# Position tables: two instead of four, filled in long rows from one tile

## The chip, the cores and the metric

The kernel runs on one core of a Trainium2 chip. The metric is the time of one execution on the device in microseconds (us), as the median of some runs. All inputs lie in the chip's memory (DRAM below); the core works from its on-chip memory (SBUF, 128 partitions) and the accumulators of the matrix engine (PSUM). Its engines are PE (matrix multiplication), DVE (vector), ACT (activation), POOL (general) and SP (which here issues DMA transfers). Sixteen DMA engines move the data.

## What is computed

Three steps on 4608 tokens (8 batches of 576):

```
attn_out = attention of q on p', where p' = attention of the 32 packed queries p on k, v
x = silu(attn_out @ w_in) @ w_out          # 512 -> 2048 -> 512
# top-1 mixture of 8 experts
e_idx = argmax(x @ w_gate)                 # one expert for each token
out[token] = gate_w * sigmoid(x @ w_output_gate)[e_idx] * (relu(x @ w1[e_idx]) @ w2[e_idx])
```

The last step gathers the tokens of one expert. That needs a list, made on the chip, of which token stands at which place.

## The kernel before

**Batches.** `batch(b)` runs over the 16 hidden slices f of the middle layer: `mm1` (L664) computes a slice, `act` (L673, L674) applies the activation, `split_hi` and `split_lo` (L679, L684) split it into a coarse and a fine part, and `mm2` (L715) multiplies with `w_out` two slices later. Between these steps the attention of the next batch is run by `att_steps` (s1 to s9; s3 is the product with v at L579, and L581 scales it). The code of `batch` is the order of the instructions on every engine; nothing is moved by a planner, and each engine runs its own instructions strictly in that order.

**First batch.** `w_in` and `w_out` come as 64-bit words and are converted during batch 0: `f64_load` (L432) loads 512 KB into a tile of tag stg, and `f64_conv` does three DVE operations on it (L452, L455, L458), for `w_out` into a tile of tag wf with two buffers, which ACT and POOL then split (L469, L470). A load reuses a stg buffer when DVE has read it. `load_att` (L524) fetches k, v and q of the next batch; the second half of v, for batch 1, is issued in step 5 and used by s3 in step 7.

**Position tables.** Four tables `perm` in DRAM hold, for each of 8 x 36 x 128 places (and 128 spare ones), one row of 16 integers, the first of which counts. `setup_late`, in batch 0 after step 4, fills each table: the first with 4608, the others with 0. The source is a tile of 289 columns, broadcast 16 times for each partition; the first table has a tile of its own, the other three share one, both of tag wf. Each fill is one DMA on SP's queue of 2312 KB (2048 rows of 1156 bytes). A row of zeros (`zrow`) is written to the end of `xr`, the rows of x in DRAM.

**Scatters.** After the routing of a group of 4 or 5 blocks of 128 tokens, `put` (L782) writes, on POOL's queue, the token numbers of each block to the places computed for them. Block i goes to table i % 4, so a scatter follows another to the same table after three others. The value written is the token for table 0, and the token less 4608 for the others.

**Gathers.** In the expert stage 38 pairs of a block of places and an expert run one after the other. `fetch_ix` reads, on SP, the 128 places of a block from all four tables into `xix_p`, and POOL adds the four (L911, L912). The sum is the token, or 4608 for an empty place, which points to the row of zeros. `fetch_x` (L920) gathers the rows of x, and `trx` (L948) transposes them on PE. The first three pairs fetch early, in batch 7; pairs 3 to 5 fetch after the last block is placed.

**Queues.** SP issues its DMAs in order through eight semaphores in turn, so each waits until the eighth before it has landed. In the rows of the order below a DMA's waits stand in brackets: DMAHW0 to DMAHW7 are those eight semaphores, DMASW0 to DMASW7 those of POOL's DMAs, and an engine's name its own progress.

Of the kernel before, what the change touches and what calls it, by code (L numbers as in the profile page):

```python
# [8 lines left out]
F32 = mybir.dt.float32  # L9
# [3 lines left out]
I32 = mybir.dt.int32  # L13
ALU = mybir.AluOpType
# [10 lines left out]
E8 = 8  # L25
F2 = 1024
NTOK = B * S
NBLK = NTOK // 128
CAP = NBLK
NPAIR = NBLK + E8 - 1  # L30
XW = DM + 1
# [3 lines left out]
HS = S // 2  # L35
EARLY = 3
NSTATIC = NBLK + 2
NPERM = 4
PW = 16


def constants():
    p = np.arange(128)
    c = np.zeros((128, C_END), np.float32)
    c[:, C_ID:C_ID + 128] = np.eye(128)
    e = np.arange(E8)
    c[:, C_E:C_E + E8] = e
    c[:, C_OFF:C_OFF + E8] = (e - E8) * CAP
    c[:, C_LT:C_LT + E8 * E8] = (e[None, :] < e[:, None]).reshape(1, -1)
    c[:, C_J] = p  # L50
    k = np.full((128, 256), 0x3F80, np.uint16)
    k[:, :128] *= p[:, None] < p[None, :]
    t = np.stack([block_tokens(i) for i in range(NBLK)], axis=1).astype(np.int32)
    t[:, np.arange(NBLK) % NPERM > 0] -= NTOK
    t = np.concatenate([t, np.zeros((128, PW - 1), np.int32)], axis=1)
    return {"cst": c, "cstk": k, "cstt": t}

# [9 lines left out]
def block_tokens(i):  # L67
    return np.concatenate([np.arange(t, t + n) for _, t, n in block_spans(i)])
# [13 lines left out]
class Kernel:  # L82
    def __init__(self, tc, ins, out):
# [3 lines left out]
        self.ws2 = nc.dram_tensor("ws2", (E8, 4, 2, 128, 2 * DM), F32, kind="Internal").ap()  # L87
        self.perm = [nc.dram_tensor(f"perm{i}", ((E8 * CAP + 1) * 128, PW), I32, kind="Internal").ap() for i in range(NPERM)]
        self.xr = nc.dram_tensor("xr", (NTOK + 1, XW), F32, kind="Internal").ap()
# [76 lines left out]
    def setup_late(self):  # L166
        nc = self.nc
        nc.sync.dma_start(self.tri, self.i["cstk"].bitcast(BF16).rearrange("p (a b) -> p a b", a=2))
        nc.sync.dma_start(self.tok, self.i["cstt"])
        nc.gpsimd.memset(self.nt_run, 0.0)  # L170
        for i, perm in enumerate(self.perm):
            if i < 2:
                fill = self.stg.tile([128, E8 * CAP + 1], I32, tag="wf", bufs=2, name="fill")
                nc.gpsimd.memset(fill, 0 if i else NTOK)
            nc.sync.dma_start(perm.rearrange("(p c) w -> p (c w)", p=128).rearrange("p (w c) -> p w c", w=PW),
                              fill.unsqueeze(1).to_broadcast([128, PW, E8 * CAP + 1]))
        z = self.rt.tile([128, 5, XW], F32, tag="xr", name="zrow")[:1, 0]
        nc.gpsimd.memset(z, 0.0)
        nc.sync.dma_start(self.xr[NTOK:NTOK + 1, :], z)

    def pick(self):
        assert self.group is None and not self.late
# [575 lines left out]
    def place(self, g):  # L758
# [15 lines left out]
        def put():  # L774
# [6 lines left out]
            for r in range(n):  # L781
                nc.gpsimd.indirect_dma_start(  # L782
                    out=self.perm[(i0 + r) % NPERM], out_offset=bass.IndirectOffsetOnAxis(ap=di[:, r:r + 1], axis=0),
                    in_=self.tok[:, i0 + r:i0 + r + PW], in_offset=None)
# [114 lines left out]
    def fetch_ix(self, j):  # L899
        nc = self.nc  # L900
        if j < EARLY:
            off = nc.values_load(self.ptab[0:1, 1 + j:2 + j], engines=[ENG.SP], min_val=0, max_val=E8 * CAP * 128)
            self.ex[j] = self.estar
        else:
            off = nc.values_load(self.tab[0:1, 0, j:j + 1], engines=[ENG.SP], min_val=0, max_val=E8 * CAP * 128)
            self.ex[j] = nc.values_load(self.tab[0:1, 1, j:j + 1], engines=[ENG.SP], min_val=0, max_val=E8 - 1)
        ix = self.rt.tile([128, NPERM + 2], I32, tag="xix_p", bufs=4, name="xix_p")
        at = self.rt.tile([128, 1], I32, tag="xix", bufs=6, name="xix")
        for i, perm in enumerate(self.perm):
            nc.sync.dma_start(ix[:, i:i + 1], perm[bass.ds(off, 128), 0:1])  # L910
        nc.gpsimd.tensor_tensor(out=ix[:, 4:6], in0=ix[:, 0:2], in1=ix[:, 2:4], op=ALU.add)  # L911
        nc.gpsimd.tensor_tensor(out=at, in0=ix[:, 4:5], in1=ix[:, 5:6], op=ALU.add)  # L912
        return at.bitcast(U32)

    def flag(self, j):
# [100 lines left out]
def layouts(q, k, v, p, moe_w_in, moe_w_out, moe2_w_gate, moe2_w_output_gate, moe2_w1, moe2_w2):  # L1016
    def headmajor(x):
        return np.ascontiguousarray(x.reshape(B, 4, 2, S, D).transpose(0, 2, 4, 1, 3).reshape(B, 128, 4, S))

    vv = np.zeros((B, 640, H, D), v.dtype)  # L1020
    vv[:, :S] = v.transpose(0, 2, 1, 3)
    vv = vv.reshape(B, 5, 128, 4, 2, D).transpose(0, 4, 2, 1, 3, 5)
    return {
        "q": headmajor(q), "k": headmajor(k), "v": np.ascontiguousarray(vv).reshape(B, 2, 128, 5, 256),
        "p": np.ascontiguousarray(p.reshape(B, 4, 2, NP, D).transpose(0, 2, 4, 1, 3)).reshape(B, 128, 4, NP),
        "w_in": np.ascontiguousarray(moe_w_in).view(np.int64), "w_out": np.ascontiguousarray(moe_w_out).view(np.int64),
        "wgt": np.ascontiguousarray(moe2_w_gate.reshape(4, 128, E8).transpose(1, 0, 2)), "wog": np.ascontiguousarray(moe2_w_output_gate.T),
        "w1": np.ascontiguousarray(moe2_w1), "w2": np.ascontiguousarray(moe2_w2),
        **constants(),
    }  # L1030
# [19 lines left out]
```

## Time and profile before

| | |
|---|---|
| median of 3 runs | 1361.1 us (1360.93 to 1362.29) |
| profiled execution | 1360.51 us, of which the span of the instructions is 1358.7 us |
| PE busy | 1269.3 us (93% of the span) |
| DVE, ACT, POOL busy | 653.9, 505.8, 173.4 us |
| granted clock of PE, mean | 0.971 |

Times in the rows below are us from the span's start. A granted clock of 1.00 is PE's full speed (2.4 GHz), 0.50 half of it (1.2 GHz). A matmul counts as busy from its start to its modelled end. The share of the DMA engines is the mean busy share of the sixteen and can exceed 1 a little.

### The profile page before, as it was taken

What the parts mean: (1) busy time and instruction counts of PE and PEld (TensorE: products, weight loads), DVE (VectorE), ACT (ScalarE), POOL (GpSimd) and SP (SyncE); (2) the same over time, 40 slices, a digit from 0 to 9 for tenths busy, and PEclk for the clock granted to TensorE, in tenths of its full rate; (3) what the DMA queues carried; (4) which work ended last, traced back from release to release, by engine and by line L of the source; (5) the groups of instructions that cost most, each with busy time, mean ns of one, the idle gap of its engine ahead of it and who ended that gap; (6) DMA issues with size and microseconds to landing.
All of it is one profiled execution on the core that took longest, in us unless ns stands there. A gap on an engine that the chain in (4) does not pass through costs nothing. (4 is left out here: it accounts for less than half of the span.)

```text
span 1358.7 us, 24463 instructions
## 1 busy us (share of the span) xinstructions
PE 1269.3 (93%) x8414; PEld 1020.1 (75%) x8416; DVE 653.9 (48%) x1417; ACT 505.8 (37%) x980; POOL 173.4 (13%) x236
## 2 busy tenths in 40 slices
PE   7754699999999899999999999999999999999997
PEld 3543578778788688787787788878888888888886
DVE  6953965845865745857556745232222222222221
ACT  3321255445464444454454433223223222222322
POOL 0220310100010100101000111112212212211210
PEclk9686899999999999999999999999999999999999
DMA  7598346846695855776665414442557383722630
GB/s 292 205 233 210 110 151 222 274 158 223 211 292 180 257 197 189 227 285 209 225 219 193 104 32 157 108 127 71 193 173 249 121 301 97 277 66 69 236 129 23
DMA packets 118303, 247.72 MB, mean 182 GB/s; under 512 B 30177, under 2 KB 56609, under 8 KB 118178
## 3 DMA queue, kind: packets, MB, share of 16 engines
q1 hardware_dynamic: 110946, 226.35, 51.0%
q0 software_dynamic: 7232, 19.72, 4.4%
q8 instruction: 77, 1.26, 0.4%
q14 instruction: 48, 0.39, 0.1%
HBM read 401.92 MB, written 96.29 MB: 367 GB/s over the span
## 5 line engine op out<-in xcount | busy, mean ns | idle before, releaser
L715 PE MATMUL acc<-wo,ghi 128*128 128x512 f32 x1024 | 320.9, 395 | 0.0
L715 PEld LDWEIGHTS acc<-wo,ghi 128*128 128x128 f32 x1024 | 194.5, 190 | 39.0
L664 PE MATMUL ps_h<-a,m_hi 128*128 128x288 f32 x1024 | 215.5, 303 | 0.8 <-DVE a L630 0.8
L715 PE MATMUL acc<-wo,glo 128*128 128x512 f32 x512 | 212.9, 416 | 0.0
L664 PE MATMUL ps_h<-a,m_lo 128*128 128x288 f32 x512 | 163.5, 319 | 30.9 <-DVE g L674 25.2
L1007 PE MATMUL py<-queue_q_buf,hhi 128*128 x608 | 190.7, 395 | 0.0
L979 PE MATMUL pu<-queue_q_buf,xhi 128*128 x560 | 174.6, 393 | 0.0
L664 PEld LDWEIGHTS ps_h<-a,m_hi 128*128 128x128 f32 x1024 | 171.1, 196 | 2.7 <-DVE a L630 1.0
L993 DVE TENSOR_TENSOR hlo<-ph,hhi 128x512 fp32r<-128x512 f32 x76 | 49.0, 686 | 247.3 <-ACT hhi L992 247.3
L674 DVE SCALAR_TENSOR_TENSOR g<-g,ps_h 128x576 f32<-128x576 f32 x128 | 96.1, 751 | 131.0 <-ACT g L673 130.2
L673 ACT ACTIVATE g<-ps_h 128x576 f32<-128x576 f32 x128 | 83.3, 651 | 188.8 <-PE ps_h L664 186.0
L664 PEld LDWEIGHTS ps_h<-a,m_lo 128*128 128x128 f32 x512 | 99.8, 195 | 57.0 <-DVE g L674 33.3
L1007 PEld LDWEIGHTS py<-queue_q_buf,hhi 128*128 128x128 f32 x608 | 114.5, 188 | 25.6
L715 PEld LDWEIGHTS acc<-wo,glo 128*128 128x128 f32 x512 | 97.3, 190 | 43.0 <-issue 24.8
L1007 PE MATMUL py<-queue_q_buf,hlo 128*128 x304 | 122.9, 404 | 0.0
L979 PEld LDWEIGHTS pu<-queue_q_buf,xhi 128*128 128x128 f32 x560 | 105.3, 188 | 22.4
L782 POOL DMA_INDIRECT perm<-tok,dsti x36 | 38.9, 1081 | 647.9 <-DVE dsti L779 507.4
L679 ACT CAST ghi<-g 128x512 fp32r<-128x512 f32 x128 | 79.4, 620 | 107.6 <-DVE g L674 106.5
L979 PE MATMUL pu<-queue_q_buf,xlo 128*128 x280 | 113.7, 406 | 0.3 <-ACT hs L981 0.3
L981 ACT ACTIVATE hs<-pu 128x512 f32<-128x512 f32 x76 | 45.4, 598 | 164.2 <-PE pu L979 162.5
L684 DVE TENSOR_TENSOR glo<-g,ghi 128x512 fp32r<-128x512 f32 x128 | 88.5, 692 | 31.1 <-ACT ghi L679 26.2
L1012 POOL DMA_INDIRECT out<-y,xix x38 | 38.2, 1006 | 328.2 <-ACT y L1010 320.6
(183 smaller groups left out, 1501.1 us busy)
## 6 DMA issues: line engine op xcount, KB each, us to landing
queue_q_buf<-ws SPq DMA_DIRECT2D x70, 4096.0 KB
ws<-shi SPq DMA_DIRECT2D x64, 512.0 KB
mid<-in_w SPq DMA_DIRECT2D x48, 512.0 KB
ws<-mid SPq DMA_DIRECT2D x48, 512.0 KB
att_v<-in_v SPq DMA_DIRECT2D x15, 640.0 KB
perm<-fill SPq DMA_DIRECT2D x4, 2312.0 KB
og<-in_wog SPq DMA_DIRECT2D x35, 256.0 KB
att_k<-in_k SPq DMA_DIRECT2D x15, 576.0 KB
```

The costliest lines, as they stand in the source:

```text
L664: nc.tensor.matmul(ps[:, hf, :288], lw[:, qd, fs], rx[:, qd, ts], start=(i == 0), stop=(i == 5))
L673: nc.scalar.activation(out=g2, in_=ps[:, :, :288], func=AF.Tanh, scale=0.5)
L674: nc.vector.scalar_tensor_tensor(out=g2, in0=g2, scalar=1.0, in1=ps[:, :, :288], op0=ALU.add, op1=ALU.mult)
L679: self.nc.scalar.copy(out=hi, in_=self.graw[:, :512])
L684: self.nc.vector.tensor_tensor(out=lo, in0=self.graw[:, :512], in1=self.ghi.bitcast(F32), op=ALU.subtract)
L715: self.nc.tensor.matmul(acc, l, r, start=(first and i == 0), stop=(last and i == 2))
L782: nc.gpsimd.indirect_dma_start(out=self.perm[(i0 + r) % NPERM], out_offset=bass.IndirectOffsetOnAxis(ap=di[:, r:r + 1], axis=0), in_=self. ...
L979: nc.tensor.matmul(ps, l[:, ks], w[:, k, r, ns], start=(i == 0), stop=(i == 11))
L981: nc.scalar.activation(out=self.hs[j][:, n * 512:n * 512 + 512], in_=ps, func=AF.Relu)
L993: nc.vector.tensor_tensor(out=lo[:, n], in0=ps, in1=hi[:, n].bitcast(F32), op=ALU.subtract)
L1007: nc.tensor.matmul(ps, l[:, k // 4, ks], w[:, k // 2, r, (k % 2) * DM:(k % 2) * DM + DM], start=(i == 0), stop=(i == 23))
L1012: nc.gpsimd.indirect_dma_start(out=self.out, out_offset=bass.IndirectOffsetOnAxis(ap=ix[:, 0:1], axis=0), in_=y, in_offset=None, bounds_ch ...
```

## The change

There are two tables instead of four. Both are filled with 2304 (half of 4608) from one tile of 2312 columns that lies in the buffer of tag xr, so each partition writes 2 rows of 9248 bytes to each table (256 rows for a table). All token numbers are written less 2304, so that the sum of the two tables is the token, or 4608. The row of zeros is taken from the tile `zero` that the kernel holds already. Block i goes to table i % 2, and a gather reads two columns and adds them once.

```diff
-NPERM = 4
+NPERM = 2
...
-    t[:, np.arange(NBLK) % NPERM > 0] -= NTOK
+    t -= NTOK // NPERM
...
-        for i, perm in enumerate(self.perm):
-            if i < 2:
-                fill = self.stg.tile([128, E8 * CAP + 1], I32, tag="wf", bufs=2, name="fill")
-                nc.gpsimd.memset(fill, 0 if i else NTOK)
-            nc.sync.dma_start(perm.rearrange("(p c) w -> p (c w)", p=128).rearrange("p (w c) -> p w c", w=PW),
-                              fill.unsqueeze(1).to_broadcast([128, PW, E8 * CAP + 1]))
-        z = self.rt.tile([128, 5, XW], F32, tag="xr", name="zrow")[:1, 0]
-        nc.gpsimd.memset(z, 0.0)
-        nc.sync.dma_start(self.xr[NTOK:NTOK + 1, :], z)
+        n = (E8 * CAP + 1) * PW // 2
+        fill = self.rt.tile([128, 5 * XW], I32, tag="xr", name="fill")[:, :n]
+        nc.gpsimd.memset(fill, NTOK // NPERM)
+        for perm in self.perm:
+            nc.sync.dma_start(perm.rearrange("(p c) w -> p (c w)", p=128).rearrange("p (h n) -> p h n", h=2),
+                              fill.unsqueeze(1).to_broadcast([128, 2, n]))
+        nc.sync.dma_start(self.xr[NTOK:NTOK + 1, :].rearrange("o (p c) -> (o p) c", p=3), self.zero.bitcast(F32)[:3, :XW // 3])
...
-        ix = self.rt.tile([128, NPERM + 2], I32, tag="xix_p", bufs=4, name="xix_p")
+        ix = self.rt.tile([128, NPERM], I32, tag="xix_p", bufs=4, name="xix_p")
...
-        nc.gpsimd.tensor_tensor(out=ix[:, 4:6], in0=ix[:, 0:2], in1=ix[:, 2:4], op=ALU.add)
-        nc.gpsimd.tensor_tensor(out=at, in0=ix[:, 4:5], in1=ix[:, 5:6], op=ALU.add)
+        nc.gpsimd.tensor_tensor(out=at, in0=ix[:, 0:1], in1=ix[:, 1:2], op=ALU.add)
```

The lines of the changed kernel stand two lower from `setup_late` on (L430 for L432) and three lower from `fetch_ix` on (L917 for L920).

On SP, in batch 0 after step 4, this stands in a row before (perm is a table, stg a buffer of the weight loads, att_v the v of the next batch):

```order
37 L175 DMA perm<-fill 2048x1x289 [waits DMAHW4_49,Pool_49]
38 L175 DMA perm<-fill 2048x1x289 [waits DMAHW5_49,Pool_49]
39 L175 DMA perm<-fill 2048x1x289 [waits DMAHW6_49]
40 L175 DMA perm<-fill 2048x1x289 [waits DMAHW7_49]
41 L179 DMA xr<-zrow 1x513 [waits DMAHW0_49,Pool_49]
42 L432 DMA stg_401<-in_w_out 128x1024 [waits DMAHW1_49,DVE_49]
43 L432 DMA stg_401<-in_w_in 128x1024 [waits DMAHW2_49,DVE_49]
44 L524 DMA att_v<-in_v 128x1280 [waits DMAHW3_49,PE_49]
45 L432 DMA stg_401<-in_w_out 128x1024 [waits DMAHW4_49,DVE_49]
46 L432 DMA stg_401<-in_w_in 128x1024 [waits DMAHW5_49,DVE_49]
47 L432 DMA stg<-in_w_out 128x1024 [waits DMAHW6_49,DVE_49]
48 L432 DMA stg<-in_w_in 128x1024 [waits DMAHW7_49,DVE_49]
```

And in the changed kernel at the same place:

```order
37 L175 DMA perm<-fill 256x1x2312 [waits DMAHW4_49,Pool_49]
38 L175 DMA perm<-fill 256x1x2312 [waits DMAHW5_49]
39 L177 DMA xr<-zero 3x171 [waits DMAHW6_49]
40 L430 DMA stg_401<-in_w_out 128x1024 [waits DMAHW7_49,DVE_49]
41 L430 DMA stg_401<-in_w_in 128x1024 [waits DMAHW0_49,DVE_49]
42 L522 DMA att_v<-in_v 128x1280 [waits DMAHW1_49,PE_49]
43 L430 DMA stg_401<-in_w_out 128x1024 [waits DMAHW2_49,DVE_49]
```

Two fills are gone, the rows of those left are eight times as long, and att_v stands two places earlier behind them.

On POOL, at the start of the expert stage, the last two groups of blocks are scattered before the first list of the late pairs is added up (perm0 to perm3 are the tables, dsti the places of a group; the branch belongs to a loop over buffers):

```order
L782 DMA perm3<-tok_91,dsti_8436 36992x16 [waits DMASW6_49,DVE_49]
L782 DMA perm0<-tok_91,dsti_8436 36992x16 [waits DMASW7_49,DMASW3_49]
L782 DMA perm1<-tok_91,dsti_8436 36992x16 [waits DMASW4_49,DMASW0_49]
L782 DMA perm2<-tok_91,dsti_8436 36992x16 [waits DMASW5_49,DMASW1_49]
L935 UNCONDITIONAL_BRANCH
L782 DMA perm3<-tok_91,dsti_8575 36992x16 [waits DMASW2_49,DVE_49]
L911 TENSOR_TENSOR xix_p_8694<-xix_p_8694 128x2 [waits DMAHW6_49,DMAHW7_49,DMAHW1_49,DMAHW0_49]
L912 TENSOR_TENSOR xix_8695<-xix_p_8694 128x1 [waits Pool_49]
```

In the changed kernel:

```order
L780 DMA perm1<-tok_91,dsti_8421 36992x16 [waits DMASW0_49,DVE_49]
L780 DMA perm0<-tok_91,dsti_8421 36992x16 [waits DMASW3_49,DMASW1_49]
L932 UNCONDITIONAL_BRANCH
L780 DMA perm1<-tok_91,dsti_8421 36992x16 [waits DMASW4_49,DMASW2_49]
L780 DMA perm0<-tok_91,dsti_8421 36992x16 [waits DMASW5_49,DMASW3_49]
L780 DMA perm1<-tok_91,dsti_8560 36992x16 [waits DMASW4_49,DVE_49]
L909 TENSOR_TENSOR xix_8680<-xix_p_8679 128x1 [waits DMAHW7_49,DMAHW6_49]
```

The scatters stand in the same order but alternate between two tables, so the third, fourth and fifth each follow one to the same table two places ahead, and one of the two additions is gone.

## Rows read from the trace of the kernel before

**Rows 1.** Five stages: length, engines' busy us (instructions), PE clock, DMA share, GB/s.

```profile
68.00:84.00 16.00, 6.15 (x71) 5.02 (x69) 2.76 (x4) 1.39 (x3) 1.69 (x5) 0.82 1.04 239
84.00:103.00 19.00, 12.65 (x69) 9.86 (x69) 17.16 (x25) 6.39 (x14) 6.28 (x6) 0.86 1.10 228
103.00:123.00 20.00, 1.37 (x41) 1.23 (x41) 0.48 (x2) 0.00 (x0) 0.00 (x0) 0.50 1.06 260
123.00:180.00 57.00, 45.75 (x289) 35.17 (x290) 49.11 (x69) 19.80 (x40) 21.47 (x19) 0.88 0.35 118
180.00:1300.00 1120.00, 1102.65 (x7319) 896.37 (x7318) 518.46 (x1203) 441.56 (x852) 123.83 (x178) 1.00 0.56 186
```

**Rows 2.** Waits, 68 to 128 us: total us, times, longest.

```profile
PE ps_s L579 <- DMA att_v<-in_v: 21.2, 1, 21.2
```

**Rows 3.** Timeline of DVE in batch 0: start, us, engine, line, operation, [idle before].

```profile
67.42 2.30 DVE L569 TENSOR_SCALAR sm<-sm 128x2 f32<-128x2 f32 x1
...
83.09 0.43 DVE L452 TENSOR_SCALAR wf<-stg 128x512 uint32<-128x512 uint32 x1 [13.17 <-DMA perm<-fill]
...
89.20 0.69 DVE L458 SCALAR_TENSOR_TENSOR w_in<-stg,w_in 128x512 uint32<-128x512 uint32 x1
...
102.78 0.69 DVE L458 SCALAR_TENSOR_TENSOR w_in<-stg,w_in 128x512 uint32<-128x512 uint32 x1
122.99 0.28 DVE L581 TENSOR_SCALAR pp<-ps_s,sm 128x64 f32<-128x64 f32 x1 [19.52 <-PE ps_s L579]
...
126.89 0.75 DVE L674 SCALAR_TENSOR_TENSOR g<-g,ps_h 128x576 f32<-128x576 f32 x1 [1.83 <-ACT g L673]
```

**Rows 4.** Timeline of PE, step 7 to step 8 of batch 0.

```profile
99.80 0.61 PE L715 MATMUL acc<-wo,ghi 128*128 128x512 f32 x2
121.63 1.30 PE L579 MATMUL ps_s<-att_v,a1t 128*32 128x64 f32 x40 [21.21 <-DMA att_v<-in_v]
```

**Rows 5.** Timeline of SP's queue in batch 0: us is the issue alone.

```profile
68.99 23.88 SPq L175 DMA_DIRECT2D perm<-fill  x4
...
104.98 0.56 SPq L524 DMA_DIRECT2D att_v<-in_v  x1
...
117.82 0.33 SPq L432 DMA_DIRECT2D stg<-in_w_in  x1
```

**Rows 6.** Stretches under the fills, under 4 KB rows, under the xr rows.

```profile
70.00:116.00 46.00, 16.80 (x127) 13.08 (x125) 18.51 (x26) 7.04 (x15) 6.28 (x6) 0.74 1.10 223
190.00:195.00 5.00, 5.00 (x41) 3.93 (x41) 2.65 (x5) 4.17 (x9) 0.00 (x0) 1.00 1.05 419
824.00:828.00 4.00, 4.00 (x34) 3.41 (x33) 1.94 (x7) 1.42 (x3) 0.00 (x0) 1.00 0.96 258
```

**Rows 7.** By line: ns min/median/max, first to last start; two tiles' memsets, L569.

```profile
L174 POOL MEMSET fill<- x2: 348/348/349, 68.6 to 68.9; 128x289 int32 x2
...
L178 POOL MEMSET zrow<- x1: 522/522/522, 69.2 to 69.2; 1x513 f32 x1
...
L569 DVE TENSOR_SCALAR sm<-sm x8: 160/166/2297, 11.3 to 700.9; 128x2 f32<-128x2 f32 x8
```

**Rows 8.** Timeline of POOL, SP and PE, start of the experts.

```profile
869.23 0.96 POOL L782 DMA_INDIRECT perm<-tok,dsti  x1 [35.55 <-DVE dsti L779]
...
873.01 0.96 POOL L782 DMA_INDIRECT perm<-tok,dsti  x1 [0.31 <-issue]
...
881.96 0.95 POOL L782 DMA_INDIRECT perm<-tok,dsti  x1 [7.99 <-DVE dsti L779]
892.09 2.09 SPq L910 DMA_DIRECT2D xix_p<-perm  x4
...
900.15 0.63 PE L948 MATMUL px<-cst,x 128*128 128x128 f32 x4 [1.18 <-DVE hlo L993]
```

**Rows 9.** L782 by line: from issue to landing, whole span; then 868 to 880 us.

```profile
DMA to landing us min/median/max: 4.7/6.2/9.5
...
DMA to landing us min/median/max: 8.8/8.9/9.0
```

## Prediction

> **What bounds the kernel now.** I read the busy time by stage first [rows 1]. From 180 to 1300 us PE is busy for 1102.65 of 1120 us at a granted clock of 1.00: what is saved on SP, POOL or the DMA engines there is worth nothing unless PE waits for it. Before 180 us the kernel is in the first batch, and PE is not the bound. In 84 to 103 us DVE is busy for 17.16 of 19.00 us; in 103 to 123 us no engine does anything (PE 1.37, DVE 0.48 of 20 us) while the DMA engines are at a share of 1.06. So the reader should see two holes in the first batch, with a stretch between them and one after them in which DVE is the bound (49.11 of 57 us in 123 to 180).
>
> The waits and the DVE timeline name both [rows 2, 3]. The first hole: L452 starts at 83.09 after 13.17 us of idling, released by the landing of a fill. It writes a buffer of tag wf, and the two fill tiles have taken buffers of that tag. The second: PE finishes its accumulations of step 7 at 100.41 (99.80 and 0.61) and waits 21.21 us, to 121.63, for att_v [rows 4]; DVE, whose next work is L581 on that result, idles for 19.52 us, and 1.83 us more before L674.
>
> Why att_v is late is on the SP queue [rows 5]. The four fills are issued from 68.99 on, and SP is held for 23.88 us by that alone. att_v goes out at 104.98. The stg load at 117.82 could go only when the fourth fill had landed (in the order of SP it waits for the semaphore that this fill posts), so I put the end of the fills at 117.3; att_v, with the 1.0 MB of stg loads ahead of it, lands 4.3 us behind, at 121.6. The holes thus have one cause: 4 x 2312 KB of stores, written at 223 GB/s over 70 to 116 us while the engines' share is 1.10 [rows 6].
>
> **The change, part by part.**
>
> *The wf buffers.* The fill no longer takes one. L450, as L452 is called now, waits for its own source and POOL only, and both were there. DVE idle: minus 13.2 us.
>
> *The fill tile.* One POOL memset of 128x2312 takes the place of two of 128x289 (348 ns each) and one of 1x513 (522 ns) [rows 7]. From 289 to 513 columns the price grows by 174 ns, 0.78 ns a column; from 2312 columns I get 348 + 2023 x 0.78 = 1.9 us, an estimate from these rows. The three old memsets end at 69.7, the new one would end at 68.7 + 1.9 = 70.6. This is not free: L569, a 128x2 operation whose median is 166 ns, lasts 2.30 us there and ends at 69.72, when POOL's last memset ends [rows 3, 7]. I read it as held by POOL, so DVE gets free 1.0 us later. Bounds: 0 (if it was something else) and plus 1.5. I take plus 1.0. SP also starts the fills at about 70.7 instead of 68.99; that goes into the next term.
>
> *The fills.* 2 x 2312 KB = 4.73 MB instead of 9.47. The rate with rows of 9248 bytes stands in no row. The nearest: stores with rows of 1156 bytes, 223 GB/s, and of 2052 bytes (the xr rows, 1.03 MB in 4.00 us), 258 GB/s, both at a share near 1; 4 KB rows, stores and loads mixed, 419 GB/s [rows 6]. As time per row, the old fills took 46.5 us (70.8 to 117.3) / 8192 = 5.7 ns and the xr rows 4.0 us / 512 = 7.8 ns: a line through both gives 3.0 ns a row and 2.3 ps a byte, so 9248 bytes would take 24.6 ns and 512 rows 12.6 us (376 GB/s). The bounds are 223 and 419 GB/s, 21.2 and 11.3 us; I take 12.6, nearer to the 4 KB rows, because what the two slow rows share is a short row.
>
> When is att_v there? DVE gets to L452 at 70.9 (69.9, where it began to idle, and 1.0) instead of 83.09, so all of the DVE-bound stretch moves up by 12.2 us. SP can issue att_v once DVE's L458 (89.20 + 0.69 before, 77.7 now) has freed the stg buffer of the load ahead of it: about 78.4, inside the fills. The old fills, issued at 68.99, were moving some 2 us later; the new ones, issued at 70.7, would run from about 72.7 to 85.3, and att_v land 4.3 us later (as now: 117.3 to 121.6), at 89.6. PE asks for it at 100.41 - 12.2 = 88.2. DVE, though, has work to 102.78 + 0.69 - 12.2 = 91.3 [rows 3], and then 1.9 us of conversion before L674, so PE may start as late as 89.6 without any cost (1.3 us for L579, 1.6 for the next step at full clock, 0.7 for ACT). The stall comes out between 0 and 1 us; I take 0.8 left of 19.52 + 1.83 = 21.35. DVE idle: minus 20.5 us. With 223 GB/s the landing moves to 98.2, and 8.6 us of stall stay.
>
> The Trainium skill speaks against this term: by its page "DMA: Bandwidth & Descriptors", sections Specifications and Why small descriptors are slow, a transfer runs at line rate from 512 bytes on, and each packet costs about 3 cycles beside one per 32 bytes. By that, rows of 1156 bytes would already be within 8% of rows of 9248 (my estimate from its figures: 36 cycles and 3), and this term would shrink by 7.8 us. The rows of 223 and 419 GB/s [rows 6] disagree with it here, unless it is the bytes of a store that are slow; that is the first rival below.
>
> *The zero row.* It loses its POOL memset (in the numbers above) and its wait on POOL. Three short rows on the DMA engines: nothing.
>
> *Two tables.* Each scatter (L782) now waits for the last but one instead of the last but four. In batches 1 to 6 POOL has nothing else after it and nobody waits for the table. The last two groups matter [rows 8, 9]: four scatters at 869.23 to 873.01, landing 8.8 to 9.0 us after issue, then one at 881.96, and SP reads the tables at 892.09. Now the third goes at about 878.2, the fourth at 879.5. The fifth needs the third to have landed: 884.4 (at 6.2 us, the median of all scatters) to 887.2 (at 9.0), and lands itself 6.2 to 9.0 us later, at 890.6 to 896.2. The reads are delayed by 0 to 4 us. Against that the first lists need 2 reads instead of 4 (2.09 us of issue, so 1.0 less) and one POOL addition instead of two, and PE waits 1.18 us at 900.15 behind this chain. So this place gives minus 1.2 to plus 3.0 us; I take 0. The fetches of the early pairs in batch 7 are delayed too, but their rows are used twelve steps of that batch later.
>
> *Fewer reads.* 76 fewer on SP and 38 fewer additions on POOL: beside a PE that is busy for 1102.65 of 1120 us, nothing.
>
> **The sum** is made against the profiled execution, 1360.5 us (span 1358.7); the median of the runs is 1361.1. 1360.5 - 13.2 + 1.0 - 20.5 + 0 = 1327.8. I say 1328. From 123 us on the first batch is DVE-bound and then PE-bound, so nothing that I see takes the shift back.
>
> **The rivals.**
>
> *The fills stay slow by the byte.* If stores to this table run at 223 GB/s whatever the row, att_v lands at 98.2 and 8.6 us of stall remain where I put 0.8: 1336. For it: 2052-byte rows reach only 258. Against: 4 KB rows at 419. The page of the Trainium skill named above would have it so, that there is nothing to win by the row.
>
> *The scatters become the bound at the start of the experts.* The chain of [rows 8] at its upper end, beside the forecast: plus 3.0, and 1331. For it: 8.9 us of landing in this group. Against: the median over all scatters is 6.2 [rows 9], and at that the fifth has landed before SP asks.
>
> *Only the first hole closes.* The loads might be held by SP's buffers, not by the fills: then 1348. Against: the stall's releaser, and nothing else is on the DMA engines in 103 to 116 us.
>
> *Slower.* att_v stands in the queue behind the whole fill. Rows of 9 KB would have to be so slow that the stall left exceeds the 12.2 + 21.35 us won, that is, it lands after 89.6 + 33.6 = 123.2: 4.73 MB in 46.2 us (72.7 to 118.9), 102 GB/s. At 90 GB/s it would be 1367. No stage with stores runs below 223.
>
> **How the numbers follow.** Forecast 0.70, fills slow by the byte 0.15, scatters 0.08, first hole only 0.05, slower 0.02. The forecast's own range is 1324 to 1331 (all of the 21.35, the faster start of the experts and a quicker clock at one end; 2 us more of stall at the other). With the slow fills in, the range is 1323 to 1338: what lies outside is the fourth and fifth case and some of the edges. About 0.2% (2.7 us) is what a measurement of this kernel can tell from no change; faster by more than that holds in all cases but the last: 0.97, within 0.01, slower 0.02.
>
> **What would show it.** In the profile after: no idle of L450 before its first conversion behind the fill, and the 128x2 operation ahead of it lasting some 3.3 us; SP held for about 1 us by two fills; a DMA share near 1 from 73 to 85 us at over 350 GB/s; PE's wait for att_v at 1 to 2 us where it was 21.2; the first batch over 33 us earlier; the distance from the start of the steady stretch to the end unchanged within 2 us; scatters 6 to 9 us apart in pairs. I am wrong if the fills still take 20 us, or if a new wait of DVE or PE stands between 90 and 180 us.

## The result, and the profile after

The changed kernel takes **1328.3 us** (median of 4 runs, 1327.8 to 1329.6) where the kernel before takes 1361.0 on the same chip: a ratio of **0.976** (95% interval 0.9743 to 0.9777), 32.7 us less. The forecast was 1328. The profiled execution is 1328.53 us long, with a span of 1326.8. One of the four executions of rows1088 below took 1770.8 us at a mean granted clock of 0.65 and is left out of its median.

Five stretches of the profile after (columns as in [rows 1]: length, busy us of PE, PEld, DVE, ACT and POOL with instructions, granted clock, DMA share, GB/s):

```profile
72.00:84.00 12.00, 8.32 (x95) 6.47 (x85) 10.42 (x16) 4.52 (x10) 4.22 (x4) 1.00 1.01 392
74.00:86.00 12.00, 8.58 (x56) 6.23 (x56) 11.04 (x17) 3.88 (x9) 3.83 (x4) 1.00 1.00 384
84.00:92.00 8.00, 5.80 (x61) 4.41 (x62) 7.46 (x12) 1.87 (x4) 2.08 (x2) 0.87 1.03 400
112.00:130.00 18.00, 11.27 (x75) 7.75 (x74) 17.31 (x22) 6.05 (x13) 8.58 (x7) 0.95 0.05 18
147.00:1267.00 1120.00, 1103.43 (x7321) 897.35 (x7320) 518.92 (x1203) 441.08 (x852) 118.32 (x143) 1.00 0.55 186
```

Under the fills the DMA engines are as full as before (a share near 1) but move 384 to 400 GB/s instead of 223 [rows 6], and DVE is busy for 87 to 93% of these stretches. The steady 1120 us, shifted by 33, are what they were in [rows 1]. And in 112 to 130 us the DMA engines now have almost nothing to do, which the experiments use.

DVE in batch 0 (start, us, engine, line, operation, [idle before]); L567, L450, L579 and L672 are L569, L452, L581 and L674 of before [rows 3]:

```profile
67.09 1.25 DVE L567 TENSOR_SCALAR sm<-sm 128x2 f32<-128x2 f32 x1
...
68.46 2.15 DVE L450 TENSOR_SCALAR wf<-stg 128x512 uint32<-128x512 uint32 x1
70.65 0.69 DVE L453 SCALAR_TENSOR_TENSOR wf<-stg,wf 128x512 uint32<-128x512 uint32 x1
...
90.87 0.28 DVE L579 TENSOR_SCALAR pp<-ps_s,sm 128x64 f32<-128x64 f32 x1 [0.28 <-PE ps_s L577]
...
94.58 0.76 DVE L672 SCALAR_TENSOR_TENSOR g<-g,ps_h 128x576 f32<-128x576 f32 x1 [1.63 <-ACT g L671]
```

POOL at the same time, with the memset of the fill tile:

```profile
66.80 1.52 POOL L468 TENSOR_TENSOR wo<-wf,wo 128x512 fp32r<-128x512 f32 x1 [1.36 <-ACT wo L467]
...
68.30 2.03 POOL L173 MEMSET fill<- 128x2312 int32 x1
```

The 13.17 us ahead of L450 are gone. L450 itself lasts 2.15 us where its median is 0.42, and ends at 70.61, 0.3 us after the memset. L567 ends at 68.34, when POOL's subtraction L468 does (68.32). Of the second hole, 0.28 and 1.63 us are left.

PE, and SP's queue, around att_v ([rows 4], [rows 5]):

```profile
86.91 0.61 PE L713 MATMUL acc<-wo,ghi 128*128 128x512 f32 x2
89.73 1.10 PE L577 MATMUL ps_s<-att_v,a1t 128*32 128x64 f32 x40 [2.20 <-DMA att_v<-in_v]
```

```profile
70.36 1.29 SPq L175 DMA_DIRECT2D perm<-fill  x2
...
77.46 1.26 SPq L522 DMA_DIRECT2D att_v<-in_v  x1
```

att_v goes out 27.5 us earlier than before and PE waits 2.20 us for it, not 21.21.

POOL at the start of the experts, with the scatters alternating between two tables [rows 8]:

```profile
837.38 0.96 POOL L780 DMA_INDIRECT perm<-tok,dsti  x1 [32.70 <-DVE dsti L777]
838.64 0.96 POOL L780 DMA_INDIRECT perm<-tok,dsti  x1 [0.30 <-issue]
845.66 0.96 POOL L780 DMA_INDIRECT perm<-tok,dsti  x1 [6.07 <-DMA perm<-tok,dsti]
847.59 0.96 POOL L780 DMA_INDIRECT perm<-tok,dsti  x1 [0.97 <-DMA perm<-tok,dsti]
852.91 0.95 POOL L780 DMA_INDIRECT perm<-tok,dsti  x1 [4.36 <-DMA perm<-tok,dsti]
```

The new waits are there (6.07, 0.97, 4.36 us), but SP reads the tables 22.6 us after the first scatter (860.01) where it did so after 22.9 (892.09 - 869.23), and from the second scatter to the end of the span are 488.2 us in both kernels. PE waits 0.35 us there instead of 1.18.

### The profile page after: what moved, and what is told of

Its sections match the earlier page's. It is cut to its first block, busy times and chain, and to the rows that moved or that the text cites. A ratio compares the mean times of both kernels' runs of the same rounds, so it can differ in the third digit from the quotient of the medians.

```text
span 1326.8 us, 24153 instructions
## 1 busy us (share of the span) xinstructions
PE 1262.3 (95%) x8414; PEld 1016.0 (77%) x8416; DVE 655.2 (49%) x1417; ACT 505.4 (38%) x980; POOL 167.7 (13%) x196
## 5 line engine op out<-in xcount | busy, mean ns | idle before, releaser
L662 PE MATMUL ps_h<-a,m_hi 128*128 128x288 f32 x1024 | 212.2, 300 | 0.8 <-DVE a L628 0.8
L662 PE MATMUL ps_h<-a,m_lo 128*128 128x288 f32 x512 | 162.3, 317 | 22.6 <-DVE g L672 16.9
L672 DVE SCALAR_TENSOR_TENSOR g<-g,ps_h 128x576 f32<-128x576 f32 x128 | 96.2, 751 | 130.1 <-ACT g L671 129.4
```

What stands on the lines that cost most here:

```text
L662: nc.tensor.matmul(ps[:, hf, :288], lw[:, qd, fs], rx[:, qd, ts], start=(i == 0), stop=(i == 5))
L672: nc.vector.scalar_tensor_tensor(out=g2, in0=g2, scalar=1.0, in1=ps[:, :, :288], op0=ALU.add, op1=ALU.mult)
```

## The experiments

Times are medians; every kernel ran beside the kernel before on its chip (1361.5, 1363.5 and 1361.0 us for the three sets of four below). "att_v" is when PE starts L577 (L579 in shift4 and shift32, L580 in short4), and the last column is what the DMA engines move in that stretch.

| kernel | time | att_v | stretch 74 to 86 us |
|---|---|---|---|
| changed | 1328.3 | 89.73 | 384 GB/s |
| short2: two tables, rows of 1156 bytes | 1340.1 | 100.62 | 224 |
| rows1088: rows of 1088 at multiples of 64 bytes | 1331.7 | 91.74 | 342 |
| shift32: the same, 32 bytes on | 1332.0 | 92.17 | 336 |
| shift4: the same, 4 bytes on | 1341.9 | 102.16 | 209 |
| long4: four tables, rows of 9248 | 1342.4 | 101.26 | 416 |
| short4: as before, wf buffers free | 1361.1 | 120.83 | 224 |

### Is it the row or the bytes?

**short2**: the changed kernel with the old rows.

```diff
-  ... rearrange("p (h n) -> p h n", h=2), fill.unsqueeze(1).to_broadcast([128, 2, n])
+  ... rearrange("p (h n) -> p h n", h=16), fill[:, :2 * n // 16].unsqueeze(1).to_broadcast([128, 16, 2 * n // 16])
```

> The changed kernel with its two fills written again in 2048 rows of 1156 bytes (the first 289 columns of the same tile, broadcast 16 times); the tile, its memset and the bytes stay. My theory (the time goes by the row, 5.7 ns for one of 1156 bytes): 4096 rows take 23.3 us instead of some 12.6, att_v lands some 10.7 us later, at about 100.4 us, PE waits about 13 us for it where the changed kernel waits 2.2, and the time is 1328.3 + 10.7 = 1339. Rival (a store is slowed only once much more than 4.7 MB is under way, as in the kernel before, so half the bytes alone brought the gain): att_v lands by 91 us and the time is 1328 to 1330.

Measured: 1340.1 us (1339.8 to 1340.8), ratio 0.9846 (0.9829 to 0.9862); att_v 10.9 us later than in the changed kernel. The same bytes in short rows are slow:

```profile
74.00:86.00 12.00, 10.07 (x59) 7.73 (x57) 11.04 (x16) 4.35 (x10) 4.19 (x4) 0.86 1.10 224
```

So half the tables, and half the bytes, don't carry the whole gain alone. **long4** turns it round:

```diff
-NPERM = 2
+NPERM = 4
-    t -= NTOK // NPERM
+    t -= NTOK - NTOK // NPERM
+        nc.gpsimd.tensor_tensor(out=ix[:, 4:6], in0=ix[:, 0:2], in1=ix[:, 2:4], op=ALU.add)
```

> The changed kernel with four tables again (each filled with 1152, tokens less 3456, block i to table i % 4, gathers of four columns and two additions), but in rows of 9248 bytes from the one tile. My theory (24.6 ns for a row of 9248 bytes): 1024 rows take 25.2 us, att_v lands 12.6 us later than in the changed kernel, and the time is about 1341; the start of the experts moves by less than 2 us. Rival (the rows alone carry the gain, the number of tables is hidden): 1328 to 1331.

Measured: 1342.4 us (1342.0 to 1343.7), ratio 0.9864 (0.9848 to 0.9881). att_v comes 11.5 us later for 4.73 MB more, 411 GB/s, and the stretch agrees:

```profile
74.00:86.00 12.00, 10.12 (x58) 7.71 (x57) 10.90 (x16) 4.59 (x11) 4.19 (x4) 0.83 1.01 416
```

A fill is worth its own time at its own rate, since att_v waits for the last one. The two halves of the change don't add up: from before, two tables alone give 21 us, long rows alone 19, and both 33. Each about halves the time of the fills, so what the second one saves is half of a half.

### Is it the row's length, or where it starts?

**rows1088**: rows about as short as the old ones, each at a multiple of 64 bytes from the table's start (a partition's 18496 bytes are 17 x 1088).

```diff
-  ... h=2), fill.unsqueeze(1).to_broadcast([128, 2, n])
+  ... h=17), fill[:, :2 * n // 17].unsqueeze(1).to_broadcast([128, 17, 2 * n // 17])
```

> The changed kernel with each fill in 17 rows of 1088 bytes for a partition instead of 2 of 9248: nearly the length of the old rows (1156), but each row starts at a multiple of 64 bytes, which 1156 doesn't give. My theory (length of the row decides; 3.0 ns a row and 2.3 ps a byte): 4352 rows of 5.5 ns take 23.9 us, PE waits about 13.5 us for att_v, and the time is about 1339.6, as for rows of 1156. Rival (where a row starts decides): the fills take 12 to 14 us, PE waits 2 to 4 us and the time is 1328 to 1330.

Measured: 1331.7 us (1329.8 to 1332.7), ratio 0.978 (0.976 to 0.9799). My theory (1339.6) falls: rows of 1088 bytes are nearly as quick as those of 9248, and the rival's 1328 to 1330 is 2 us short.

```profile
74.00:86.00 12.00, 8.58 (x57) 6.25 (x57) 11.04 (x17) 4.03 (x9) 3.99 (x4) 1.00 1.09 342
```

But 1156 differs from 1088 in length too. **shift4** and **shift32** keep 4352 rows of 1088 bytes and move the whole filled stretch by s = 1 or 8 numbers:

```diff
-  "perm{i}", ((E8 * CAP + 1) * 128, PW)
+  "perm{i}", ((E8 * CAP + 1) * 128 + 1, PW)
+  flat = perm.rearrange("c w -> (c w)")
+  nc.sync.dma_start(flat[s:s + 256 * n].rearrange("(p h n) -> p h n", p=128, h=17), ...)
+  nc.sync.dma_start(flat[:s].unsqueeze(0), fill[:1, :s])
```

> Rows of 1088 bytes, 17 for a partition, as in rows1088, but the whole filled stretch begins 4 bytes later in each table (the table has one row more, and a DMA of 4 bytes fills the first number). Length, count and bytes of the rows are those of rows1088; only where they start and end is off the multiples of 64 bytes. If the place decides: the stretch 74 to 86 us runs near the 220 to 250 GB/s of short2, PE waits 11 to 13 us for att_v and the time is 1338 to 1341. If it is something else about 1156 (its length, not a multiple of 64): about 355 GB/s and 1331, as rows1088.

> As shift4, but the stretch begins 32 bytes later: rows of 1088 bytes at 32 above a multiple of 64. If a multiple of 64 is what a row needs: as shift4, 1338 to 1341. If a multiple of 32 is enough: as rows1088, about 355 GB/s and 1331. In the changed kernel every second row starts there, but with 9248 bytes a row it has few starts to pay for.

Measured: 1341.9 us (1341.2 to 1342.8; ratio 0.9847, 0.9831 to 0.9863) with 4 bytes, 1332.0 us (1329.6 to 1332.5; 0.9769, 0.9753 to 0.9786) with 32. shift4, then shift32:

```profile
74.00:86.00 12.00, 8.58 (x58) 6.26 (x57) 11.04 (x17) 4.09 (x9) 4.05 (x4) 1.00 1.13 209
```

```profile
74.00:86.00 12.00, 10.09 (x59) 7.80 (x58) 11.04 (x16) 4.43 (x10) 4.19 (x4) 0.86 1.13 336
```

Same rows, same count, same source; shifting by 4 bytes costs 10 us, by 32 bytes nothing. Where the row lies decides, and a multiple of 32 is enough; shifts of 8 or 16 bytes were not tried. 1156 is 4 above such a multiple, so seven of eight old rows started off it; 9248 is 289 x 32, so none of the new ones does. The Trainium skill, page "Collectives: The Full Stack", section Rules for kernel authors, asks for buffers aligned to 32 bytes, for collectives, because that "Prevents HW read-modify-write". The number agrees with these stores (336 GB/s against 209); the mechanism no run here shows. Nor was it told apart whether the start or the end of a row matters: both were moved.

Sizes: long4 gives 22.5 ns for a row of 9248 bytes (11.53 us / 512), so the fills of the changed kernel take some 11.5 us. rows1088 takes 2.0 us more, 13.5 us or 3.1 ns a row; shift4 12.4 more, 23.9 us or 5.5 ns a row; short2 22.4 us or 5.5 ns. A row off the multiples of 32 thus costs 2.4 ns more; a row in place costs 0.5 ns and 2.4 ps a byte. These are estimates from when PE starts on att_v; the first fill goes out at 70.4 to 70.8 us in these runs, so each time is good to some 0.4 us.

### One hole or two?

**short4**: the kernel before, with the fill tiles moved out of the wf buffers (and the row of zeros taken from the tile `zero`).

```diff
-                fill = self.stg.tile([128, E8 * CAP + 1], I32, tag="wf", bufs=2, name="fill")
+        ft = self.rt.tile([128, 5 * XW], I32, tag="xr", name="fill")
+        fa, fb = ft[:, :c], ft[:, c:2 * c]
```

> The kernel before, four tables in rows of 1156 bytes, with only the fill tiles moved from the two wf buffers to the buffer of tag xr (and the row of zeros from the tile of zeros). The two holes have one cause, so my theory is that nothing is won: L452 (of before) no longer idles 13 us, DVE and PE reach the second hole 12 to 13 us earlier, but att_v still lands behind all four fills at about 122 us, and the hole grows from 21 to about 34 us: 1360 to 1362. Rival (the terms of my sum stand each for itself, minus 13.2 and plus 0 to 1): 1348 to 1349.

Measured: 1361.1 us (1360.4 to 1364.5), ratio 1.000 (0.999 to 1.001). L452's idle is gone, and all of it stands again behind att_v: DVE idles for 32.61 us there, where the two holes of before were 13.17 and 19.52.

```profile
122.18 0.28 DVE L582 TENSOR_SCALAR pp<-ps_s,sm 128x64 f32<-128x64 f32 x1 [32.61 <-PE ps_s L580]
...
120.83 1.30 PE L580 MATMUL ps_s<-att_v,a1t 128*32 128x64 f32 x40 [32.77 <-DMA att_v<-in_v]
```

### Where the fills stand

**late** moves the set-up to step 10, before the DMA engines' empty 18 us; **late_short4** does so with short4.

```diff
-            if b == 0 and f == 4:
+            if b == 0 and f == 10:
                 self.setup_late()
```

> The changed kernel with the whole of the position tables' set-up moved from after step 4 of batch 0 to after step 10, where the DMA engines are at a share of 0.01 to 0.10 (112 to 130 us). att_v then has no fill ahead of it. My theory (all that the fills still cost is the wait for att_v, 2.2 us of PE, 1.9 us of DVE): 1328.3 - 1.9 = 1326.4, PE's wait for att_v under 0.5 us; POOL's memset holds DVE there as here, 1.7 us. Rival (the loads of the next batches, now behind the fills, come late): a new wait of 2 to 10 us between 112 and 160 us, 1328 to 1336.

> Four tables in rows of 1156 bytes as before (fill tiles in the xr buffer), but the set-up moved to after step 10 of batch 0, as in late. The fills still take some 46 us, from about 113 to 159. My theory (where the fills stand in the queue decides what they cost, not only how long they are): both holes of the kernel before are gone, and the loads of the next batch, behind the fills, come some 10 us late at 150: 1326.4 + 0 to 12, so 1327 to 1338, 1334 as one number. Rival (46 us of stores must be paid wherever they stand): 1355 to 1362.

late: 1325.4 us (1324.3 to 1325.6), ratio 0.9722 (0.9706 to 0.9738). No wait for att_v is left, and the memset, at 114.81 there, stands beside DVE operations of the usual length:

```profile
115.42 0.69 DVE L456 SCALAR_TENSOR_TENSOR wf<-stg,wf 128x512 uint32<-128x512 uint32 x1
116.03 0.75 DVE L672 SCALAR_TENSOR_TENSOR g<-g,ps_h 128x576 f32<-128x576 f32 x1
```

late_short4: 1345.7 us (1345.3 to 1346.4), ratio 0.9874 (0.9857 to 0.989), beyond the 1327 to 1338 that I expected. The old holes are gone, but 46 us of slow stores don't fit into the gap. Its waits, 140 to 170 us (total, times, longest):

```profile
PE ps_s L536 <- DMA att_k<-in_k: 14.7, 1, 14.7
```

and the stretch of 25 us behind it:

```profile
145.00:170.00 25.00, 10.25 (x73) 7.80 (x72) 3.35 (x7) 3.77 (x7) 1.18 (x2) 0.69 1.08 251
```

I had counted 10 us by which the next batch's loads come late; PE waits 14.7 us, and the granted clock, 0.69 over these 25 us, stands at 0.50 from 160 to 170 us. How the rest divides, no run tells. Each against the kernel before on its own chip: moving the old fills away wins 18 us, shortening them in place 33, both 36 to 38.

### What is left beside the changed kernel

**after2** is the changed kernel, **late2** late again.

> The changed kernel once more, unedited, as the base for the three beside it on this chip: 0.976 of the kernel before, 1328 to 1331.

> The kernel of late once more beside the changed kernel. In late, DVE's 1.9 us of waiting behind att_v was gone and POOL's memset of 2.03 us stood beside DVE operations that it did not lengthen (0.69 and 0.75 us, as elsewhere), where in the changed kernel L450 lasts 2.15 instead of 0.42 us beside it. My theory: 1.9 + 1.7 less than the changed kernel, so 3.0 to 3.6 us faster. Rival (only the wait for att_v counts): 1.9.

after2: 1327.4 us (1326.7 to 1329.1; ratio 0.975, 0.9737 to 0.9764). late2: 1324.6 us (1324.5 to 1325.5; 0.9731, 0.9718 to 0.9745). The runs don't overlap; late2 is 2.8 us faster, between the two theories. In its profile the first scatter starts 4.0 us earlier (216.35 for 220.37), but the profiled execution of after2 is the slowest of its five (1329.1 us), so this doesn't decide between them. late is the fastest kernel here but for late_dve, from which it can't be told.

**actfill** takes the memset from POOL.

```diff
-        nc.gpsimd.memset(fill, NTOK // NPERM)
+        nc.gpsimd.memset(one, NTOK // NPERM)
+        nc.scalar.copy(out=fill, in_=one.to_broadcast([128, n]))
```

> The changed kernel, set-up in its place after step 4, but the tile of 2312 columns is written by ACT (a copy of one column, broadcast), so that POOL doesn't hold DVE. My theory: L450 falls from 2.15 to about 0.42 us, but nothing is won, since PE then only asks for att_v 1.7 us sooner and att_v's landing is set by the fills: 0 to 1 us slower than the changed kernel, PE's wait for att_v 3.5 to 5 us. Rival (the hold is a cost of its own): 1.7 us faster.

Measured: 1330.9 us (1328.5 to 1332.4), ratio 0.9772 (0.9759 to 0.9786). L450 (here L452) is short again, and PE still starts at 90.26, as in after2:

```profile
68.14 0.43 DVE L452 TENSOR_SCALAR wf<-stg 128x512 uint32<-128x512 uint32 x1
```

```profile
90.26 0.77 PE L579 MATMUL ps_s<-att_v,a1t 128*32 128x64 f32 x40 [3.96 <-DMA att_v<-in_v]
```

That part is as expected. But it is 3.5 us slower than after2, not 0 to 1, though the runs overlap a little (1328.5 to 1332.4 and 1326.7 to 1329.1). At the first scatter 1.2 us of that is there (221.55 for 220.37); at the end of batch 0 PE has a granted clock of 0.88 in 140 to 150 us (1.00 in after2). The rest stays open.

**late_dve** gives POOL's subtraction L468 to DVE, in late.

```diff
-        self.nc.gpsimd.tensor_tensor(out=self.wo[1][:, f, :], in0=w,
+        self.nc.vector.tensor_tensor(out=self.wo[1][:, f, :], in0=w,
```

> late, with the subtraction that makes the fine part of w_out (L468, 1.5 us on POOL) moved to DVE. In the changed kernel L453, 0.69 us alone, lasts 1.54 to 1.67 us where POOL's L468 runs beside it, some 12 times in the DVE-bound part of batch 0. If POOL holds DVE there, DVE pays 0.97 us for each; doing the work itself it would pay 0.69: 12 x 0.28 = 3.4 us faster than late, 1 to 4 with what DVE may then wait for ACT. Rival (the long L453 has another cause): 12 x 0.69 = 8 us slower than late.

Measured: 1324.5 us (1323.4 to 1325.7), ratio 0.9729 (0.9716 to 0.9742): as late2. POOL's L468 is what lengthens L453; one form of it by line (ns min/median/max), in the changed kernel and in late_dve:

```profile
L453 DVE SCALAR_TENSOR_TENSOR w_in<-stg,w_in x16: 678/693/1671, 9.6 to 113.5; 128x512 uint32<-128x512 uint32 x16
```

```profile
L453 DVE SCALAR_TENSOR_TENSOR w_in<-stg,w_in x16: 679/692/694, 10.7 to 109.5; 128x512 uint32<-128x512 uint32 x16
```

Both theories missed the total. At one L672 (124.08 for 125.44) DVE is 1.4 us ahead of late2; at the one of 147.72 (147.02 in late2) it has idled 2.18 us for ACT and is 0.7 us behind. What DVE wins is lost again at the end of batch 0, where PE is the bound: it is busy for all of 138 to 150 us, in late2 too.

## Why the prediction was right, step by step

**One cause, two holes**: right, and shown by short4. But my terms of 13.2 and 20.5 us don't stand for themselves: with the first hole alone closed nothing is won. The rival "only the first hole closes" was priced wrongly, at 1348; short4, which closes that hole alone, takes 1361.

**The wf buffers and the memset**: L450 ends at 70.61 where L452 ended at 83.52, 12.9 us earlier; forecast were 12.2. The memset took 2.03 us (estimate 1.9). It held a DVE operation, as said, but in this profile not the one I named: L567 went from 2.30 to 1.25 us, not to 3.3, and L450 took the hold. In the profiles of short2, long4 and shift32 the memset did hold L567, and L450 was short (0.42 us). Here is short2:

```profile
67.27 3.28 DVE L567 TENSOR_SCALAR sm<-sm 128x2 f32<-128x2 f32 x1
```

So which of the two operations is held differs between these profiles, with the same instructions up to there. I also overlooked POOL's subtraction: before, it ran beside L569 to 68.64, ahead of the memsets, so not all of the 2.30 us was the memsets' doing. The Trainium skill, page "SBUF — State Buffer", section Who interferes with whom, has a POOL instruction block DVE operations with one SBUF input when they run in a two-port mode, and those with two inputs when POOL reads SBUF. The rows agree as far as they go: L450 (one input) is held by the memset, L456 in late (two) is not, and L453 (two) is held by L468, which reads. In which mode L450 runs no row shows.

**The fills**: the term was right in size and wrong in cause. Forecast: 12.6 us, att_v at 89.6; measured: 11.5 and 89.7. The line of 3.0 ns a row and 2.3 ps a byte has the right slope, 2.4, but 2.4 of the 3.0 ns are paid for where a row lies. The step that failed is "what the two slow rows share is a short row": 1156 and 2052 bytes also share that they are 4 above a multiple of 32. With 9248 bytes a row the 3.0 ns hardly counted, so the error didn't show: even off the multiples, long rows would take 22.5 + 2.4 = 24.9 ns by my estimate, 12.7 us in all. That the landing came out to 0.1 us is luck. The fills were 1.1 us quicker and went out 0.3 us earlier than I said, but the rest of the way from their issue to PE's start on att_v took some 7.9 us (89.73 - 70.36 - 11.5), where I counted 2 + 4.3. At 11.5 us against 22.4, the rows are worth 10.9 us of landing; about 9 of it is the place.

**The rule weighed in the prediction**: by the Trainium skill, page "DMA: Bandwidth & Descriptors", section Specifications, 512 bytes are enough. That would have been wrong for rows of 1156 (5.5 ns) and nearly right for rows of 1088 in place: 3.1 ns, where 1088/9248 of a long row is 2.65. Taken by itself it says nothing of where the row lies.

**The stall that was left**: 1.9 us of DVE idle, not 0.8. DVE came 0.7 us earlier to the same landing, so the two misses nearly cancel: 12.2 + 20.5 = 32.7 us forecast, 12.9 + 19.4 = 32.3 measured, and 31.9 in the spans. Of the signs, two were missed by little: PE's wait was 2.20 us, not 1 to 2, and the first scatter came 32.2 us earlier, where batch 0 was to end over 33 earlier.

**Two tables at the start of the experts**: 0, as taken; the third scatter follows the first after 8.3 us (forecast 9.0) and the fifth after 15.5 (15.2 to 18.0). **Zero row, fewer reads, the steady stretch**: nothing, as said; from the first scatter on, 1106.9 us remain where 1106.6 did (1326.8 - 219.85, 1358.7 - 252.07).

**The rivals**: long4 (416 GB/s) and the rate under the fills rule out that the fills are slow by the byte; the scatters' chain ran at the low end of its price.

## What to carry to other kernels

When two holes have one cause, price the cause: see what the late transfer waits for, and sum up to its landing, not hole by hole; and before shortening a transfer, look for the nearest stretch with idle DMA engines and ask whether it fits there. When stores are slow with the DMA engines full, look at where each row begins in DRAM as well as at its length, and try a shift of a few bytes: two kinds of slow row can share more than the property that one thinks of first.

## What the runs showed of the hardware that I had not expected

- Stores to DRAM with rows at multiples of 32 bytes and those 4 bytes off ran at 336 and 209 GB/s (4352 rows of 1088 bytes, the loads beside them counted); 2.4 ns a row. The rows of xr, 2052 bytes, lie off the multiples too (258 GB/s [rows 6]). The prediction read 7.8 ns a row there, and the sizes found here give as much (0.5 + 2.4 x 2.052 + 2.4, an estimate); padding them was not tried.
- A memset of 2.03 us on POOL cost DVE 1.7 us beside an operation with one input (L450, 2.15 us for 0.42) and nothing, in late, beside one with two inputs (L456) and one with PSUM as one of two (L672).
